# Attention on 128-key value tiles: two ways to lay out keys, weights and sums in one fused kernel

## The chip, the cores and the metric

The kernel runs on one core of a Trainium2 chip. The metric is the device time of one execution in microseconds. Five engines work in parallel, each through its own queue in order: TensorE (PE, with its weight loads listed apart as PEld), VectorE (DVE), ScalarE (ACT), GpSimd (POOL) and SyncE (SP), which here only issues DMA transfers.

## The reference, cut to what matters

Threshold attention over 8 batches of 8 heads, 576 tokens and 64 columns a head, followed by a feed-forward layer with squared ReLU. All is float32.

```python
scale = 1.0 / np.sqrt(q.shape[-1])
scores = scale * np.matmul(q, k.transpose(0, 1, 3, 2))
thresh = np.max(scores, axis=-1, keepdims=True) - tau
scores = np.where(scores >= thresh, scores, -1000000000.0)
attn = np.exp(scores - np.max(scores, axis=-1, keepdims=True))
attn = attn / (np.sum(attn, axis=-1, keepdims=True) + 1e-09)
x = np.matmul(attn, v)          # (B,H,S,D), then to (B*S, H*D) = 4608 x 512
h = np.maximum(x @ w_in, 0.0)   # w_in 512 x 2048
out = h * h @ w_out             # w_out 2048 x 512
```

## The kernel before, in words

The kernel has two stages. The first, about 520 us long, is the attention, and beside it the weights of the layer are loaded and combined. The second is the feed-forward layer, two dense matrix products written as two-level fast multiplication with 7 x 7 block products in place of 8 x 8. The change touches only the first stage.

**Units and periods.** Heads are taken in 32 pairs (`pairs`), the two heads j = 0, 1 of a pair side by side. A unit is 128 queries of a pair: four full units (t = 0 to 3) of 128 rows each, and one unit for every two pairs that holds the last 64 queries of both. That makes 144 units, worked off two at a time, u = 0 (called A) and u = 1 (called B), in 72 periods (`period(p)`, L607). Inside a period every engine's work is issued in the order of a written list: `CONVERTING` (L596) in the periods in which a chunk of the layer's weights is also being converted (33 of them, p = 2 to 34), `PLAIN` (L592) in the others. Since each engine's queue runs in order, this list is the schedule. In PLAIN periods POOL adds the weight sums `s1` and `s2` in between.

**One unit's way.** Queries and keys are loaded in natural layout (`load_q`, `load_k`), and TensorE transposes them (`turn`, L390, step T) into PSUM banks 1 and 4. ACT evicts them (step eT): queries, and the 64 left-over queries, by an ACTIVATE with the scale `qscale` (a [128, 1] operand, minus one eighth; L402), keys by plain copies (L410). `scores` (L423, steps SA and SB) multiplies 64 head columns by 64 queries at a time, on 64 x 64 quarters of the array, into the six banks of `sc`. `softmax` (L439) then issues:

- `top` (L452, DVE): reads 576 scores of one head out of PSUM, multiplies by the constant 1.0, writes them to `s` and accumulates the minimum (the scores are negated, so it is minus the maximum). Steps topA0, topA1, topB0, topB1.
- `least` (L459, POOL): threshold = that minimum + tau, for both heads of a unit (steps leastA, leastB).
- `power` (L462, ACT): exp of the scores into `w`, which is laid out as 9 blocks of 64 keys x 2 heads x 64 keys' columns.
- `mask` (L467, DVE): keeps the weights whose score passes the threshold (a [128, 1] operand) and accumulates their sum. Steps maskA1, maskA0, maskB0, maskB1.
- `over` (POOL, L474) and `inverse` (DVE, L477, step inv): one over the sums, in the period after.

**Values.** The weights must be turned, so that keys lie on partitions. `fill` (L499) transposes 18 blocks (9 for each of the two units; steps V 8 blocks, W 2, U 8), each as two half transposes (L379), into PSUM; `filled` copies them to `wT` with ACT (L523, steps eV, eW, eU). A block has 64 keys of head 0 on partitions 0 to 63 and 64 keys of head 1 on partitions 64 to 127; keys are taken as 9 consecutive per partition row. In step W, eight small matmuls (L515) against the identity also spread the inverse sums over 64 partitions each. `values` (L525, step PV) multiplies: for each of 9 key chunks, each unit and each head, 64 keys x 64 columns of `v` by 128 queries, on 64 x 64 quarters of the array; head 0 accumulates in bank 0, head 1 in bank 5, unit u in partitions 64u to 64u + 63. A float32 matmul runs as two passes, so 36 matmuls of a period show as 72. `given_out` (step x, L638) multiplies the result by the spread inverse sums on DVE, frees the `v` tile (`load_v` then fetches that of three pairs on) and hands `x` to SP, which writes it to DRAM (L578).

**What orders PE against DVE.** `touch` (L354) adds a dependency wherever two engines use one PSUM bank. So PV, which writes banks 0 and 5, waits for topA0 and topA1 of its period; topA0 waits for T, which writes banks 1 and 4 between SA and topA0; SA waits for eT of the period before.

Of the kernel before, what the change touches and what calls it, by code (L numbers as in the profile page):

```python
# [48 lines left out]
def kernel(  # L49
# [249 lines left out]
    def load_k(i):  # L299
# [4 lines left out]
        for j in range(2):  # L304
            queue = nc.scalar if i == 0 and j == 0 else nc.sync
            keys = k[b, h + j, :, :].rearrange("(p c) d -> p c d", c=CH)
            for e in range(2):
                queue.dma_start(
                    out=kn[ds(e * HALF, HALF), :, ds(j * D, D)],
                    in_=keys[:, ds(e * FULL, FULL), :],  # L310
                )
# [3 lines left out]
            queue.dma_start(out=rn[REST:P, ds(j * D, D)], in_=keys[:, CH - 1, :])  # L315
        queue = nc.sync if i else nc.scalar
        queue.dma_start(
            out=rn[0:REST, :].rearrange("p (j d) -> p j d", j=2),
            in_=q[b, h : h + 2, MAIN:S, :].rearrange("j p d -> p j d"),
        )  # L320
        loaded[i, 1], loaded[i, 2] = kn, rn

    def load_v(i):
        b, hp = pairs[i]
        h = 2 * hp
        va = sb.tile([P, CH, D], FP32, tag="va", bufs=3, name="va")
        nc.sync.dma_start(
            out=va[:, :, :].rearrange("p c d -> p (c d)"),
            in_=v[b, h : h + 2, :, :].rearrange("j (p c) d -> (j p) (c d)", c=CH),
        )  # L330
        loaded_v[i] = va
# [58 lines left out]
    def turn(i, which, spots, other=None):  # L390
# [10 lines left out]
        def scaled(to, spot):  # L401
            touch("turned", nc.scalar.activation(out=to, in_=spot[0], func=AF.Identity, scale=qscale[:, :]), spot[1], BANK, i)  # L402

        def then():
            part = lambda r, x, n: (spots[r][0][:, ds(x, n)], spots[r][1])
            if which:
                for r, n in ((0, half), (1, half + REST)):
                    spot = part(r, 0, n)
                    copy_by = other if r and other else nc.scalar.copy
                    touch("turned", copy_by(to[1][:, ds(r * half, n)], spot[0]), spot[1], BANK, i)  # L410
                scaled(to[2], part(0, half, REST))
                next_keys(i)
            else:
                for r in range(2):
                    scaled(to[0][:, ds(r * half, half)], part(r, 0, half))
# [23 lines left out]
    def softmax(n):  # L439
# [8 lines left out]
        of = lambda j: s[:, j, :].rearrange("p (c d) -> p c d", d=D)  # L448

        def top(j):  # L450
            at = 3 * j * BANK + (n % 2 != j) * (2 * BANK - REST)
            made = nc.vector.tensor_scalar(  # L452
                out=s[:, j, :], in0=sc[:, ds(at, S)], scalar1=1.0, scalar2=None,
# [7 lines left out]
        def power(j):  # L461
            nc.scalar.activation(  # L462
                out=w[:, :, j, :], in_=of(j), func=AF.Exp, bias=nmx[:, j : j + 1], scale=-1.0
            )

        def mask(j):
            nc.vector.scalar_tensor_tensor(  # L467
                out=w[:, :, j, :], in0=of(j), scalar=thr[:, j : j + 1], in1=w[:, :, j, :],
# [23 lines left out]
    FIRST = [(u, c) for c in range(CH) for u in range(2)]  # L492
    FILLS = {"V": (0, 8), "W": (8, 2), "U": (10, 8)}
    SCALE_AT = 10

    def weight_at(n):
        return n if n < SCALE_AT else n + 2

    def fill(m, f, pt, at=None):  # L499

        first, count = FILLS[f]
        if m not in wT:
            wT[m] = sb.tile([P, (2 * CH + 2) * P], FP32, tag="wT", bufs=W_RING, name="wT")
        for i, (u, c) in enumerate(FIRST[first : first + count]):
            half_turn(pt, i, weights[2 * m + u][:, c, :, :].rearrange("p j d -> p (j d)"), at)
        if f == "W":
            rs = smalls.pop(m)
            for j in range(2):
                for r in range(2):
                    rows = ds(r * HALF, HALF)  # L510
                    for u in range(2):
                        one = rs[rows, 3, 2 * u + j : 2 * u + j + 1]
                        wide = bass.AP(tensor=one.tensor, offset=one.offset, ap=[one.ap[0], [0, D]])
                        to = pt[ds(u * D, D), r, ts(count + j, HALF)]
                        made = nc.tensor.matmul(to, wide, ident[rows, rows], start=True, stop=True)  # L515
                        touch("turns", made, at and at + r * BANK, BANK)

    def filled(m, f, pt, at=None):

        first, count = FILLS[f]  # L520
        count += 2 * (f == "W")
        to = wT[m][:, ds(weight_at(first) * P, count * P)]
        touch("weights", nc.scalar.copy(joined(to), whole(pt, 0, count)), at, 2 * BANK, m)  # L523

    def values(m):  # L525

        for c in range(CH):
            for u in range(2):
                for s, (i, _, count, row) in enumerate(halves(2 * m + u)):
                    for j in range(2):  # L530
                        rows = ds(j * D, D)
                        made = nc.tensor.matmul(  # L532
                            sc[ds(u * D, D), ds(5 * j * BANK + row, count)], loaded_v[i][rows, (c - (u != j)) % CH, :],
                            wT[m][rows, ds(weight_at(2 * c + u) * P + row, count)],
                            start=(c == 0 and s == 0), stop=(c == CH - 1), skip_group_check=True,
                        )
                        touch("values", made, 5 * j * BANK, BANK, m)
# [672 lines left out]
```

## Time and profile before

| what | value |
|---|---|
| timed runs | 1318.28, 1319.75, 1321.89 us; median 1319.75 |
| profiled execution | span 1314.0 us from first to last instruction; the page gives no time around it, and the median of the timed runs lies 5.8 us above |
| granted TensorE clock | 0.998 |
| PE / DVE / ACT / POOL busy over the span | 97% / 77% / 65% / 64% |
| DVE busy, 35.55 to 264.31 us (31 converting periods) | 225.2 of 228.8 us |
| DVE busy, 264.31 to 507.47 us (37 periods, nearly all plain) | 234.2 of 243.2 us |
| PE busy in the same two stretches | 210.8 and 239.6 us |

The two stretches are bounded by reciprocals (L477), of which there is one a period: 35.55, 264.31 and 507.47 us are starts of such instructions. Busy times count the spans of instructions, and neighbours on one engine overlap a little; where a price is wanted, the distance from one start to the next in the timeline is the better measure. Matmul ends are modelled, so a busy PE alone does not say that PE is the limit.

### The profile page before, as it was taken

Reading aid. Unit: us, or ns where it says so; the run is one execution under the profiler, and the core shown is the slowest. Engines: PE = TensorE matmul, PEld = TensorE weight load, DVE = VectorE, ACT = ScalarE, POOL = GpSimd, SP = SyncE. Lnnn points to the kernel's source line nnn. Section 1 sums busy time; section 2 is a strip of 40 time slices with the busy share of each in tenths; the row PEclk is TensorE's granted clock in tenths of the full one; section 3 lists DMA queues with packets and bytes.
Section 4 is the critical chain, followed back from the end, with each engine's and each line's share of the span. In section 5 each row is a group of like instructions: output and inputs, shape, how many; then the busy total and the mean of one; then the engine's idle time right before and its main releaser. Section 6 shows DMA issues by size and latency. Waiting matters only on the chain.

```text
span 1314.0 us, 47792 instructions
## 1 busy us (share of the span) xinstructions
PE 1277.6 (97%) x19483; PEld 1141.4 (87%) x19483; DVE 1016.3 (77%) x2497; ACT 849.6 (65%) x1464; POOL 839.0 (64%) x958
## 2 busy tenths in 40 slices
PE   7999999899999999999999999999999999999998
PEld 5666666677777777999999999999999999999998
DVE  5999999999999996877887788777656654665463
ACT  5999999888989886566756675665524322432240
POOL 1444444455555421778987888758777777777775
PEclk9999999999999999999999999999999999999999
DMA  5555566544433322466656655669645135423411
GB/s 135 143 160 142 155 174 182 149 103 99 101 78 86 77 60 46 148 206 192 195 180 210 197 187 179 193 232 394 249 161 161 48 115 162 161 63 100 161 33 33
DMA packets 247035, 192.12 MB, mean 146 GB/s; under 512 B 97184, under 2 KB 195488, under 8 KB 246816
## 3 DMA queue, kind: packets, MB, share of 16 engines
q1 hardware_dynamic: 245360, 188.63, 47.4%
q8 instruction: 153, 2.51, 0.8%
q10 hardware_dynamic: 1456, 0.44, 0.1%
q14 instruction: 66, 0.54, 0.1%
HBM read 116.65 MB, written 72.35 MB: 144 GB/s over the span
## 4 chain that ended last, share of the span: by engine, by line
PE 85%; ACT 8%; DVE 3%; issue 2%; DMA 1%; SPq 1%; POOL 0%; ACTq 0%; DVEq 0%; POOLq 0%
PE ph L812 30%; PE po L947 28%; PE sc L434 9%; PE sc L532 8%; PE pt L379 5%; ACT arena L523 3%; ACT arena L462 3%; PE sc L397 2%; PE sc L515 2%; DVE arena L452 1%; PE sc L379 1%; DMA wall<-w 1%; ACT arena L402 1%; DVE arena L467 0%; DMA arena<-in_k_dram 0%
## 5 line engine op out<-in xcount | busy, mean ns | idle before, releaser
L125 POOL TENSOR_TENSOR arena<-arena 128x512 f32<-128x512 f32 (+1 forms) x314 | 378.0, 1222 | 134.5 <-DVE arena L125 120.5
L947 PE MATMUL po<-wall,arena 128*128 128x128 f32 x3528 | 395.0, 275 | 1.6 <-ACT arena L724 1.4
L947 PEld LDWEIGHTS po<-wall,arena 128*128 128x128 f32 x3528 | 394.3, 192 | 2.2 <-ACT arena L724 1.8
L812 PE MATMUL ph<-arena,wall 128*128 128x128 f32 x3528 | 394.2, 275 | 0.7 <-DVE arena L638 0.7
L812 PEld LDWEIGHTS ph<-arena,wall 128*128 128x128 f32 x3528 | 394.0, 192 | 0.8 <-issue 0.8
L125 DVE TENSOR_TENSOR arena<-ph,arena 128x512 f32<-128x512 f32 x378 | 256.4, 689 | 86.2 <-PE ph L812 66.0
L122 POOL TENSOR_TENSOR arena<-arena 128x128 f32<-128x128 f32 (+2 forms) x314 | 255.2, 814 | 48.6 <-DMA arena<-w 31.9
L125 DVE TENSOR_TENSOR arena<-po,arena 128x128 f32<-128x128 f32 x378 | 108.4, 290 | 167.6 <-PE po L947 163.4
L467 DVE SCALAR_TENSOR_TENSOR arena<-arena 128x576 f32<-128x576 f32 x288 | 229.6, 817 | 2.7 <-ACT arena L462 1.7
L462 ACT ACTIVATE arena<-arena 128x576 f32<-128x576 f32 x288 | 208.2, 778 | 14.1 <-DVE arena L452 7.0
L452 DVE TENSOR_SCALAR_CACHE_REDUCE arena<-sc 128x576 f32<-128x576 f32 x288 | 205.5, 751 | 13.3 <-ACT arena L523 5.5
L758 ACT COPY c<-arena 128x512 f32<-128x512 f32 (+1 forms) x303 | 173.5, 579 | 50.4 <-DVE arena L122 41.3
L532 PEld LDWEIGHTS sc<-arena 64*64 64x64 f32 x5760 | 154.0, 133 | 55.3 <-DVE arena L452 28.7
L532 PE MATMUL sc<-arena 64*64 64x128 f32 (+1 forms) x5760 | 176.7, 263 | 18.1 <-DVE arena L452 11.6
L122 DVE TENSOR_TENSOR arena<-arena,c 128x512 f32<-128x512 f32 (+1 forms) x267 | 174.9, 663 | 6.1 <-ACT c L758 4.0
L434 PE MATMUL sc<-arena 64*64 64x64 f32 (+1 forms) x2304 | 167.4, 414 | 5.6 <-ACT arena L402 5.6
L523 ACT COPY arena<-pt 128x1024 f32<-128x1024 f32 x144 | 146.6, 1018 | 24.8 <-PE pt L379 24.4
L724 ACT COPY arena<-po 128x128 f32<-128x128 f32 x63 | 16.6, 264 | 186.4 <-PE po L947 183.7
L459 POOL TENSOR_SCALAR arena<-arena,tau_p 128x2 f32<-128x2 f32 x144 | 75.1, 521 | 73.4 <-DVE arena L452 67.8
L724 ACT COPY arena<-ph 128x512 f32<-128x512 f32 x63 | 36.6, 581 | 124.2 <-PE ph L812 123.5
L379 PEld LDWEIGHTS pt<-ident,arena 64*128 64x128 f32 x2304 | 83.1, 139 | 38.2 <-ACT arena L523 25.6
L434 PEld LDWEIGHTS sc<-arena 64*64 64x64 f32 x2304 | 59.2, 134 | 52.2 <-ACT arena L402 26.4
(46 smaller groups left out, 896.1 us busy)
## 6 DMA issues: line engine op xcount, KB each, us to landing
g<-arena SPq DMA_DIRECT2D x144, 256.0 KB, 2.4
arena<-g SPq DMA_DIRECT2D x144, 256.0 KB, 4.4
w<-arena SPq DMA_DIRECT2D x60, 256.0 KB, 2.4
wall<-w SPq DMA_DIRECT2D x49, 256.0 KB, 5.2
arena<-w SPq DMA_DIRECT2D x44, 256.0 KB, 3.2
arena<-in_v_dram SPq DMA_DIRECT2D x32, 288.0 KB, 3.6
out_dram<-arena SPq DMA_DIRECT2D x70, 128.0 KB, 2.2
arena<-in_q_dram SPq DMA_DIRECT2D x64, 128.0 KB, 3.2
```

The source lines that it names most:

```text
L122: e.tensor_tensor(out=out, in0=x, in1=y, op=ALU.subtract)
L125: e.tensor_tensor(out=out, in0=x, in1=y, op=ALU.add)
L379: made = nc.tensor.transpose(pt[:, r, ts(slot, HALF)], of[rows, :], ident[rows, rows])
L434: made = nc.tensor.matmul(sc[at, ds(to, count)], lhs, kT[rows, ds(at_k, count)], start=True, stop=True)
L452: made = nc.vector.tensor_scalar(out=s[:, j, :], in0=sc[:, ds(at, S)], scalar1=1.0, scalar2=None, op0=ALU.mult, op1=ALU.min, accum_out=nmx ...
L462: nc.scalar.activation(out=w[:, :, j, :], in_=of(j), func=AF.Exp, bias=nmx[:, j : j + 1], scale=-1.0)
L467: nc.vector.scalar_tensor_tensor(out=w[:, :, j, :], in0=of(j), scalar=thr[:, j : j + 1], in1=w[:, :, j, :], op0=ALU.is_le, op1=ALU.mult, a ...
L523: touch("weights", nc.scalar.copy(joined(to), whole(pt, 0, count)), at, 2 * BANK, m)
L532: made = nc.tensor.matmul(sc[ds(u * D, D), ds(5 * j * BANK + row, count)], loaded_v[i][rows, (c - (u != j)) % CH, :], wT[m][rows, ds(weigh ...
L758: nc.scalar.copy(c, y)
L812: nc.tensor.matmul(to[:, j, :], W_IN[m, k][:, ts(j, P)], of[k][:, m - 1, :], start=(not more and j == 0), stop=True, skip_group_check=True,)
L947: nc.tensor.matmul(to, g[:, j, :], w[:, j, :], start=(not more and j == 0), stop=(j == 3), skip_group_check=True)
```

## The change

Five things change together, all in the attention stage.

- **Keys over 128 partitions.** `load_k` loads keys 0 to 511 of a head as 4 consecutive keys for each of 128 partitions, in one DMA a head; the last 64 keys of both heads go beside the last 64 queries. ACT's evictions of the turned keys interleave two PSUM banks. `load_v` loads `v` in the same order: two DMAs for the main part and two for the last 64 keys, which are loaded twice, on both partition halves.
- **Weights laid out by head.** `w` is 2 heads x 576 keys, contiguous; which head comes first depends on the unit, so that the last 64 keys of both heads meet in one block of 128 columns.
- **Values of 128 keys by 64 columns.** A period turns 16 blocks of 128 keys of one head and 2 blocks with the rests of both. `values` multiplies 128 keys x 64 columns by 128 queries, on the left or right 64 columns of the array by head; the rests go on 64 x 64 quarters, in the middle (order 0, 1, rest, 2, 3). Unit u now has its own bank (0 or 5) and head j its partitions. For a period of two full units: 16 + 4 matmuls instead of 36. `x` is 128 x 256, and neighbouring query blocks of a pair go to DRAM in one DMA.
- **Sums spread by transposes of a widened copy.** A new step `spread`, right behind `inv`, has POOL write the four inverse sums of a period 64 times over (`widen`, 128 x 256); W turns these two blocks with the two rest blocks. The eight matmuls of L515 go. U stays 8 blocks, V 8, W becomes 4.
- **Scores scaled in the maximum pass.** ACT's evictions of queries are plain copies, and `top` multiplies by `qscale`, a [128, 1] operand, in place of the constant 1.0.

```diff
-        units.append(((i, i + 1), FULL))
+        units.append(((i, i + 1) if i % 4 == 0 else (i + 1, i), FULL))
...
+            queue.dma_start(
+                out=kn[:, :, ds(j * D, D)], in_=k[b, h + j, 0:MAIN, :].rearrange("(p t) d -> p t d", t=FULL)
+            )
...
+        for rows, x in ((ds(0, REST), k), (ds(REST, REST), q)):
+            queue.dma_start(
+                out=rn[rows, :].rearrange("p (j d) -> p j d", j=2),
+                in_=x[b, h : h + 2, MAIN:S, :].rearrange("j p d -> p j d"),
+            )
...
+        for j in range(2):
+            nc.sync.dma_start(
+                out=va[:, j, :, :], in_=v[b, h + j, 0:MAIN, :].rearrange("(p t) d -> p t d", t=FULL)
+            )
+        for e in range(2):
+            nc.sync.dma_start(
+                out=vr[ds(e * REST, REST), :, :], in_=v[b, h : h + 2, MAIN:S, :].rearrange("j p d -> p j d")
+            )
...
-            touch("turned", nc.scalar.activation(out=to, in_=spot[0], func=AF.Identity, scale=qscale[:, :]), spot[1], BANK, i)
+        def evicted(by, to, spot, first, n):
+            made = by(to, spot[0][:, ds(first, n)].rearrange("p (t q) -> p t q", q=HALF))
+            touch("turned", made, spot[1], BANK, i)
...
-        w = sb.tile([P, CH, 2, D], FP32, tag="w", bufs=4, name="w")
+        w = sb.tile([P, 2, S], FP32, tag="w", bufs=4, name="w")
...
-                out=s[:, j, :], in0=sc[:, ds(at, S)], scalar1=1.0, scalar2=None,
+                out=s[:, j, :], in0=sc[:, ds(at, S)], scalar1=qscale[:, :], scalar2=None,
...
-    FILLS = {"V": (0, 8), "W": (8, 2), "U": (10, 8)}
+    FILLS = {"V": (0, 8), "W": (16, 4), "U": (8, 8)}
...
+    def widen(m):
+        if m not in wT:
+            wT[m] = sb.tile([P, (SCALE_AT + 2) * P], FP32, tag="wT", bufs=W_RING, name="wT")
+        one = smalls.pop(m)[:, 3, 0:1]
+        wide = bass.AP(tensor=one.tensor, offset=one.offset, ap=[one.ap[0], [1, 4], [0, D]])
+        nc.gpsimd.tensor_copy(out=wT[m][:, ds(SCALE_AT * P, 2 * P)].rearrange("p (x d) -> p x d", d=D), in_=wide)
...
-        for c in range(CH):
+        for n, c in enumerate((0, 1, FULL, 2, 3)):
             for u in range(2):
                 for s, (i, _, count, row) in enumerate(halves(2 * m + u)):
                     for j in range(2):
+                        va, vr = loaded_v[i]
+                        if c < FULL:
+                            lhs, rhs = va[:, j, c, :], wT[m][:, ds((4 * c + 2 * j + u) * P + row, count)]
+                        else:
+                            rows = ds((u != j) * REST, REST)
+                            lhs, rhs = vr[rows, j, :], wT[m][rows, ds((TAIL + u) * P + row, count)]
                         made = nc.tensor.matmul(
-                            sc[ds(u * D, D), ds(5 * j * BANK + row, count)], loaded_v[i][rows, (c - (u != j)) % CH, :],
+                            sc[ds(j * D, D), ds(5 * u * BANK + row, count)], lhs, rhs,
...
-        inv powA0 c5 topB1 powB1 eT maskA1 x W eV maskA0 leastB c2 c6 eW maskB0 maskB1
+        inv spread powA0 c5 topB1 powB1 eT maskA1 x W eV maskA0 leastB c2 c6 eW maskB0 maskB1
...
-        leastB inv powA0 PV powB0 W maskA0 x powB1 maskB0 T c4 c5 maskB1 eT V c6 eW eV
+        leastB inv spread powA0 PV powB0 W maskA0 x powB1 maskB0 T c4 c5 maskB1 eT V c6 eW eV
```

More of the change, by code (lines that the diff above doesn't have):

```diff
@@ L544, in valued @@
             if units[n][1] == FULL:
-                for i in units[n][0]:
+                for i in sorted(units[n][0]):
                     loaded_v.pop(i)
@@ L550, in give_x @@
     def give_x(m, x):
[L552 to L557 removed]
+        for i, first, count, at in parts_of(m, lambda x, y: (x[0], x[1] + x[2]) == y):
+            b, hp = pairs[i]
+            given.append((xT[b][ds(hp * P, P), ds(first, count)], x[:, ds(at, count)]))
     def has(n):
@@ L673, in period @@
         }
+        steps["spread"] = lambda: has(2 * m + 2) and widen(m + 1)
         steps["over"] = lambda: do(a, "over")
```

101 lines of the change are left out of this document (39 added, 62 removed).

## The prediction, made before the result was known

> **What bounds the kernel now.** I read the page first, then busy time by stage, the groups by shape, and two stretches of the timeline.
>
> ```profile
> span 1314.0 us, 47792 instructions
> PE   7999999899999999999999999999999999999998
> DVE  5999999999999996877887788777656654665463
> ```
>
> PE is busy everywhere, but in the first 16 slices, the attention, DVE is as full. The change touches only these slices, so the rest of the span stays. The busy time of the two attention stretches (PE, PEld, DVE, ACT, POOL, then clock, DMA share, GB/s) tells them apart:
>
> ```profile
> 35.55:264.31 228.76, 210.78 (x5358) 146.01 (x5352) 225.22 (x654) 215.25 (x349) 102.25 (x156) 1.00 0.57 157
> 264.31:507.47 243.16, 239.59 (x6310) 179.94 (x6306) 234.21 (x702) 216.83 (x337) 118.04 (x168) 1.00 0.35 83
> ```
>
> The first holds 31 converting periods, 7.38 us each: DVE is busy for 98% and PE for 92%. The second holds 37 periods of 6.57 us: PE 99%, DVE 96%. Both engines matter, and the timeline must say which ends last. First the prices by group and shape (busy, mean ns, idle before):
>
> ```profile
> L467 DVE SCALAR_TENSOR_TENSOR arena<-arena 128x576 f32<-128x576 f32 x288 | 229.6, 817 | 2.7 <-ACT arena L462 1.7
> L452 DVE TENSOR_SCALAR_CACHE_REDUCE arena<-sc 128x576 f32<-128x576 f32 x288 | 205.5, 751 | 13.3 <-ACT arena L523 5.5 <-PE sc L397 2.0 <-ACT arena L212 1.7
> L235 DVE SCALAR_TENSOR_TENSOR arena<-arena 128x512 int32<-128x512 int32 x32 | 22.3, 698 | 1.1
> L402 ACT ACTIVATE arena<-sc,qscale 128x256 f32<-128x256 f32 x62 | 25.6, 463 | 4.2 <-PE sc L397 4.2
> L410 ACT COPY arena<-sc 128x256 f32<-128x256 f32 x32 | 11.6, 361 | 6.2 <-PE sc L397 6.2
> ```
>
> A converting period in the timeline (start, length); the distance between starts is what an instruction costs DVE:
>
> ```profile
> 147.77 0.70 DVE L235 SCALAR_TENSOR_TENSOR arena<-arena 128x512 int32<-128x512 int32 x1
> ...
> 148.38 0.82 DVE L467 SCALAR_TENSOR_TENSOR arena<-arena 128x576 f32<-128x576 f32 x1
> ...
> 149.12 0.76 DVE L452 TENSOR_SCALAR_CACHE_REDUCE arena<-sc 128x576 f32<-128x576 f32 x1
> ...
> 149.80 0.76 DVE L452 TENSOR_SCALAR_CACHE_REDUCE arena<-sc 128x576 f32<-128x576 f32 x1
> ```
>
> A top costs 0.68, a mask 0.74, L235 0.61; by the same view L227 costs 0.46, the two x multiplies 0.40, the reciprocal 0.09. A converting period's DVE work is 4 x 0.68 + 4 x 0.74 + 0.46 + 0.61 + 0.40 + 0.09 = 7.24 us of 7.38: DVE sets these periods. A plain one has 6.17 us of DVE work. There:
>
> ```profile
> 387.45 0.76 DVE L452 TENSOR_SCALAR_CACHE_REDUCE arena<-sc 128x576 f32<-128x576 f32 x1
> ...
> 388.13 0.75 DVE L452 TENSOR_SCALAR_CACHE_REDUCE arena<-sc 128x576 f32<-128x576 f32 x1
> 388.30 0.13 PEld L532 LDWEIGHTS sc<-arena 64*64 64x64 f32 x1 [0.28 <-DVE arena L452]
> 388.73 2.16 PEld L532 LDWEIGHTS sc<-arena 64*64 64x64 f32 x71 [0.30 <-issue]
> ...
> 390.45 0.81 DVE L467 SCALAR_TENSOR_TENSOR arena<-arena 128x576 f32<-128x576 f32 x1
> 390.63 0.79 POOL L459 TENSOR_SCALAR arena<-arena,tau_p 128x2 f32<-128x2 f32 x1
> 391.07 0.57 PEld L379 LDWEIGHTS pt<-ident,arena 64*128 64x128 f32 x16 [0.17 <-issue]
> ...
> 391.56 0.20 PEld L379 LDWEIGHTS sc<-ident,arena 64*128 64x128 f32 x4
> ...
> 391.83 0.32 PEld L515 LDWEIGHTS sc<-ident,arena 64*64 64x64 f32 x16
> ...
> 393.96 0.76 DVE L452 TENSOR_SCALAR_CACHE_REDUCE arena<-sc 128x576 f32<-128x576 f32 x1
> ```
>
> This is a loop: topA0, topA1, the value products (which wait for both), V, W, SA, T, and the next topA0, 387.45 to 393.96 = 6.51 us, mostly PE. DVE has 0.34 us to spare in it.
>
> **The change part by part.**
>
> *Scale in top.* L452 gets a [128, 1] operand. No such DVE instruction out of PSUM is in the trace. From below: nothing, if its fetch hides behind the PSUM read; no reason gives a gain. From above: ACT's L402 with such an operand against L410 without, both 128x256 out of PSUM, 463 - 361 = 0.10 us. Between: on DVE, L467 has the operand and L235, of the same kind, has a constant; beyond 1.04 ns an element (L125 on DVE: 689 ns at 512, 290 at 128), so 0.60 and 0.53 us, they cost 0.14 and 0.08 from start to start. I take 0.06: same engine, and 0.10 is another's. That is +0.24 us of DVE work a period, 0.12 of it (topA0, topA1) on the plain loop. The Trainium skill, "ScalarE: Activation LUTs", section What ACT_TABLE_LOAD costs, gives about 93 ns for each pointer operand of an ACTIVATE, as L402 and L410 agree; as an estimate for DVE it would put the sum about 6 us higher, but that page speaks of ACT.
>
> *Query evictions as copies.* Two of 463 become 361, and the 64-query one (324) falls likewise: about 0.3 us less ACT a pair. ACT is on the path only where scores wait for the eviction itself: one plain period in nine takes 7.09 us (356.64 to 363.73) since PE waits 0.41 for L402. There it gives back 0.2. Key evictions move as many columns.
>
> *Value products.* 72 passes ran on quarters, four together: 2.16 us for 18 slots of 0.12. After, 32 passes on half arrays go two together and 8 on quarters four together: again 18 slots. A slot of full rows is in the trace: L812, 3528 passes in 394.2 us, 0.112. So no gain by the count. The first waits fall otherwise: before, the second product already writes bank 5 and waits for topA1; after, two slots go to bank 0 first: -0.16. New are two changes of array shape, into the rests and out. PEld's idle time at such changes is 0.17 (before V at 391.07) and 0.07 (391.76 to 391.83, before L515); I take 0.12 each, between them: +0.24. Entering PV is hidden by its wait for topA1. The Trainium skill, "TensorEngine Tiling (Array Packing)", Key Properties, says that changing the tiling mode drains the engine; the 0.17 agrees in kind, and a full drain is a rival below.
>
> *Sums.* L515's 16 weight loads take 391.83 to 392.06 = 0.23 off W and a shape change 0.07, four more half transposes add 4 x 0.036 (16 in 0.57), and the change back to quarters moves to SA: W goes from 0.50 (391.56 to 392.06) to 0.36, -0.14. POOL gets `spread`, 128x256. Prices: not under 0.23 (L474, 128x4), not over 0.61 (L219, 128x512, one input); about 0.4, half way. It must end before W's last blocks and stands ahead of leastB, for which maskB0 waits. leastB at 390.63 took 0.79, against 0.29 elsewhere, because it began under maskA1. After, in plain periods with two weight sums (44 sums on `wall`, so 22 periods), the second sum ends 0.12 later, at 390.75; spread begins under maskA1 (390.69 to 391.43), ends near 391.8, and leastB then meets maskA0 (391.83 to 392.57) and ends near 392.8, while DVE wants maskB0 at 392.57. I take 0.25 of DVE wait there; the ends are 0 and leastB's full 0.79. In converting periods leastB comes first, and spread can delay only W, where PE has 0.5 us to spare.
>
> *Loads and stores.* Costed at nothing. SP issues ten transfers a pair before and after (keys 7 to 4, values 1 to 4), stores fall from 20 to 13 per four pairs, at 0.6 each; the issues of 36 to 264 us sum to 167 us, so SP has room, and values are fetched three pairs ahead. Where that cover fails, it is a key load: one 7.44 us period now ends on one. Contiguous `w`: ACT and DVE move as many elements. Not counted: neither L467 nor L462 shows a price for runs.
>
> *Sum.* Converting: DVE work 7.24 + 0.24 = 7.48; of today's 0.14 of waits I keep 0.05, as ACT gets lighter: 7.53, +0.15, for 33 periods +5.0. Plain, ordinary (29 periods): loop 6.51 + 0.12 - 0.16 + 0.24 - 0.14 = 6.57, +0.06, +1.7; DVE work is 6.41, and with leastB's wait 6.66, +0.09 more in 22 periods, +2.0. Four periods without a turn run at 6.23 to 6.29 and cannot fall under 6.41: +0.6. The four late ones: +0.12 - 0.21, -0.4. Total +8.9: span 1323; outside it stay the 5.8 us by which the median 1319.75 exceeds it: 1329.
>
> **Rivals.**
>
> *The operand is free (faster).* Place: the four tops; price 0 in place of 0.06; under about 0.02 this case decides. Converting 7.24 + 0.05: -3.0. Plain 6.45, leastB's wait no longer binding (6.17 + 0.25): -1.7, late periods -0.8. Together -5.5: 1314. For it: the trace has no such DVE read of PSUM, and a fetch from SBUF could run beside it. Against: L402 reads PSUM too and pays.
>
> *No measurable change.* Spread slips in ahead of the masks and a shape change costs 0.07: plain 6.47, -1.2 - 0.4 - 0.4 + 0.6, and half of converting's price lost in today's waits, +3: 1321. For it: in 15 plain periods POOL has no second sum.
>
> *Full drains.* Each of the two changes costs a whole matmul, 0.27 (L532's 274 ns), not 0.12: +0.30 in 33 periods, +10: 1339. This is the drain rule named above at its dearest. Against: L515 started 0.07 after its predecessor's loads.
>
> *Half arrays don't run side by side, or their loads aren't hidden.* 16 more slots of 0.112, +1.8 us: plain +66, converting (PE 6.8 to 8.6) +36: over 1420. Against: four quarters do run together, and L812's loads of all rows (394.0 us) hide fully. The skill's "TensorE: Matmul & The Clock Gate", The mechanism, lets loads overlap only where row groups differ; L812 speaks against its biting here.
>
> **How the numbers follow.** Forecast 0.41, free operand 0.20, no change 0.22, full drains 0.12, no overlap 0.05. The bound for telling a change is 0.3%, 4 us: 1315.8 and 1323.7. Faster: the free operand's 0.20. Same: 0.22 and the forecast's lower edge, 0.05: 0.27. Slower: the rest, 0.53. Range: the free operand with cheap shape changes (0.10 less, 33 times, -3.3) gives 1311, full drains with 3 us more for a dearer operand 1342; outside lie no overlap and the tails. The forecast's own range is 1323 to 1336.
>
> **What would show it.** L452's mean near 811 and starts 0.74 apart; L402's line at 361; converting periods of 7.5 us; plain ones of 6.6, with L467 idle before maskB0 on POOL L459; PV's 40 passes as long as 72 were, with a gap on either side of the rests. Tops still 0.68 apart, or value passes 0.112 apart singly, would make it wrong.

## The result, and the profile after

| | before | after |
|---|---|---|
| median of the timed runs | 1318.78 us (1315.46 to 1322.49) | 1321.76 us (1318.88 to 1327.33) |
| span of the profiled execution | 1314.0 us | 1317.1 us |
| 31 converting periods | 228.76 us | 231.92 us |
| 37 plain periods | 243.17 us | 244.02 us |
| ahead of them | 35.55 us | 34.91 us |

The ratio is 1.0023, 95% interval [1.0012, 1.0034]: 3 us slower, where 9 were forecast. Of the 3.1 us by which the span grew, converting holds +3.16, plain +0.85, the start -0.64 and all the rest -0.3. After has 40,939 instructions in its span, 6,900 fewer. The busy time of the two attention stretches of after (PE, PEld, DVE, ACT, POOL, then clock, DMA share, GB/s):

```profile
34.91:266.82 231.91, 206.47 (x3870) 137.85 (x3868) 230.16 (x652) 211.81 (x349) 129.03 (x187) 1.00 0.55 153
266.82:510.85 244.03, 241.82 (x4566) 163.25 (x4564) 239.72 (x704) 214.61 (x336) 134.33 (x205) 1.00 0.34 86
```

In converting DVE went from 225.2 to 230.2 us while the stretch grew by only 3.2: its waits shrank. PE lost 4.3 us of work there, to no effect on the time. In plain DVE gained 5.5 us and PE 2.2, and the stretch grew by 0.85. The groups of after, by shape (busy, mean ns of one | idle before):

```profile
L468 DVE SCALAR_TENSOR_TENSOR arena<-arena 128x576 f32<-128x576 f32 x288 | 228.5, 814 | 0.8 <-ACT arena L463 0.7
L453 DVE TENSOR_SCALAR_CACHE_REDUCE arena<-sc,qscale 128x576 f32<-128x576 f32 x288 | 221.8, 812 | 8.4 <-PE sc L399 2.1 <-issue 1.8 <-ACT arena L212 1.6
L404 ACT COPY arena<-sc 128x256 f32<-128x256 f32 x93 | 31.1, 368 | 7.1 <-PE sc L399 7.1
L512 POOL COPY arena<-arena 128x256 f32<-128x256 f32 x72 | 55.0, 764 | 11.9 <-DVE arena L478 8.1 <-PE sc L551 0.9
```

The top (L453, was L452) went from 751 to 812 ns, the 0.06 of the forecast, while the masks (L468) stayed at 814. Evictions of 128 x 256, queries and keys in one group now, take 368 ns; queries took 463. The copy of the sums (L512) takes 764 on average, where 0.4 us was taken. A plain period of after in the timeline:

```profile
390.18 0.82 DVE L453 TENSOR_SCALAR_CACHE_REDUCE arena<-sc,qscale 128x576 f32<-128x576 f32 x1
...
390.92 0.81 DVE L453 TENSOR_SCALAR_CACHE_REDUCE arena<-sc,qscale 128x576 f32<-128x576 f32 x1
391.51 0.92 PEld L551 LDWEIGHTS sc<-arena 128*64 128x64 f32 x16 [0.81 <-DVE arena L453]
...
392.60 0.21 PEld L551 LDWEIGHTS sc<-arena 64*64 64x64 f32 x8 [0.17 <-issue]
392.98 0.85 PEld L551 LDWEIGHTS sc<-arena 128*64 128x64 f32 x16 [0.17 <-issue]
...
393.24 0.82 DVE L468 SCALAR_TENSOR_TENSOR arena<-arena 128x576 f32<-128x576 f32 x1
393.31 1.00 POOL L512 COPY arena<-arena 128x256 f32<-128x256 f32 x1
...
394.00 0.58 PEld L381 LDWEIGHTS pt<-ident,arena 64*128 64x128 f32 x16 [0.17 <-PE sc L551]
...
394.30 0.29 POOL L460 TENSOR_SCALAR arena<-arena,tau_p 128x2 f32<-128x2 f32 x1
394.38 0.81 DVE L468 SCALAR_TENSOR_TENSOR arena<-arena 128x576 f32<-128x576 f32 x1
...
395.11 0.82 DVE L468 SCALAR_TENSOR_TENSOR arena<-arena 128x576 f32<-128x576 f32 x1
...
396.79 0.82 DVE L453 TENSOR_SCALAR_CACHE_REDUCE arena<-sc,qscale 128x576 f32<-128x576 f32 x1
```

The loop runs from 390.18 to 396.79, 6.61 us (6.51 in the period shown of before). The value products end with the transposes of V at 394.00, 2.49 us after they began. On either side of the rests PE's loads stand 0.17 idle, waiting for nothing that the profile shows; these are the places where the array shape changes. The tops start 0.74 apart. And maskB0, at 395.11, does not wait: leastB ended at 394.59.

The lengths of single periods, from one reciprocal to the next, tell more than sums. Converting: before, most lie between 7.19 and 7.45, often 7.20 and 7.33 in turn (a period that transposes keys, then one that transposes queries); after, 28 of 31 lie between 7.43 and 7.47. Plain periods come in a pattern of nine (us, in order; the second has no turn, the last waits for the query eviction):

| | 1 | 2 | 3 | 4 | 5 | 6 | 7 | 8 | 9 |
|---|---|---|---|---|---|---|---|---|---|
| before | 6.50 | 6.29 | 6.68 | 6.51 | 6.45 | 6.51 | 6.58 | 6.50 | 7.09 |
| after | 6.47 | 6.49 | 6.62 | 6.55 | 6.61 | 6.54 | 6.68 | 6.54 | 6.96 |

### The profile page after: what moved, and what is told of

The parts are those of the page before. It is cut to its first block, busy times and chain, and to the rows that moved or that the text cites. A ratio compares the mean times of both kernels' runs of the same rounds, so it can differ in the third digit from the quotient of the medians.

```text
span 1317.1 us, 40939 instructions
## 1 busy us (share of the span) xinstructions
PE 1275.0 (97%) x16059; PEld 1116.0 (85%) x16059; DVE 1027.7 (78%) x2497; ACT 843.7 (64%) x1464; POOL 883.7 (67%) x1030
## 4 chain that ended last, share of the span: by engine, by line
PE 82%; DVE 8%; ACT 5%; issue 2%; POOL 1%; DMA 1%; DVEq 0%; POOLq 0%; ACTq 0%
PE ph L828 30%; PE po L963 29%; PE sc L436 9%; PE sc L551 8%; PE pt L381 4%; DVE arena L453 4%; DVE arena L468 3%; ACT arena L463 3%; PE sc L399 1%; POOL arena L512 1%; PE sc L381 1%; ACT arena L526 1%; DVE arena L235 1%; DMA wall<-w 1%; ACT arena L404 1%
## 5 line engine op out<-in xcount | busy, mean ns | idle before, releaser
L468 DVE SCALAR_TENSOR_TENSOR arena<-arena 128x576 f32<-128x576 f32 x288 | 228.5, 814 | 0.8 <-ACT arena L463 0.7
L453 DVE TENSOR_SCALAR_CACHE_REDUCE arena<-sc,qscale 128x576 f32<-128x576 f32 x288 | 221.8, 812 | 8.4 <-PE sc L399 2.1
L551 PEld LDWEIGHTS sc<-arena 128*64 128x64 f32 (+1 forms) x3200 | 141.5, 135 | 72.7 <-DVE arena L453 45.3
L551 PE MATMUL sc<-arena 128*64 128x128 f32 (+3 forms) x3200 | 184.5, 272 | 11.7 <-DVE arena L453 10.6
L460 POOL TENSOR_SCALAR arena<-arena,tau_p 128x2 f32<-128x2 f32 x144 | 65.9, 458 | 65.5 <-DVE arena L453 61.5
L436 PEld LDWEIGHTS sc<-arena 64*64 64x64 f32 x2304 | 58.6, 134 | 53.3 <-issue 24.8
```

The costliest lines, as they stand in the source:

```text
L436: made = nc.tensor.matmul(sc[at, ds(to, count)], lhs, kT[rows, ds(at_k, count)], start=True, stop=True)
L453: made = nc.vector.tensor_scalar(out=s[:, j, :], in0=sc[:, ds(at, S)], scalar1=qscale[:, :], scalar2=None, op0=ALU.mult, op1=ALU.min, accu ...
L468: nc.vector.scalar_tensor_tensor(out=w[:, int(n % 2 != j), :], in0=s[:, j, :], scalar=thr[:, j : j + 1], in1=w[:, int(n % 2 != j), :], op0 ...
L551: made = nc.tensor.matmul(sc[ds(j * D, D), ds(5 * u * BANK + row, count)], lhs, rhs, start=(n == 0 and s == 0), stop=(n == FULL), skip_gro ...
```

## The experiments

The theory going in was the forecast's: DVE's work sets the converting periods, so the operand of the tops is their price, and the shape changes that of the plain ones. Its rival: something else, the copy of the sums above all, holds the time up. Ratios are to the kernel before, on the same chip; stretches are of one profiled execution each. In nearly every profile some converting periods between 155 and 260 us are longer than the others by 0.3 to 3.4 us, other ones each time, and the stretch ahead of the converting periods varies by up to 3.7 us. So readings rest on single periods first; sums over the converting stretch carry that noise, those over the plain one hardly.

**The operand undone (e1_scale_back), and alone (e2_scale_only).** In e1, after's tops multiply by 1.0 again and ACT scales the queries:

```diff
+        def scale(to, spot):
+            return nc.scalar.activation(out=to, in_=spot, func=AF.Identity, scale=qscale[:, :])
...
-                    evicted(nc.scalar.copy, part, spots[r], 0, half)
+                    evicted(scale, part, spots[r], 0, half)
...
-                out=s[:, j, :], in0=sc[:, ds(at, S)], scalar1=qscale[:, :], scalar2=None,
+                out=s[:, j, :], in0=sc[:, ds(at, S)], scalar1=1.0, scalar2=None,
```

> The changed kernel with one part undone: scores scaled in ACT's query evictions again, the maximum pass multiplies by the constant 1.0. Theory (each engine's own work decides: converting periods follow DVE's work, plain periods follow PE's chain): L453's starts go from 0.74 back to 0.68 us apart; converting periods fall from 7.48 to 7.3 us on average, -0.1 to -0.2 in 33 periods, so -3 to -6 us against the changed kernel; ordinary plain periods stay at 6.55 to 6.6, because PE has no wait left in them, and the plain period that waits for a query eviction grows by 0.2, +1 us in all. Together -2 to -5 us against the changed kernel, about level with the kernel before. Rival (PE's waits for the widened copy, 31 us in the converting stretch, set the converting periods): these stay at 7.44 or more and the time does not fall.

In e2, before has this one part of the change and no other:

```diff
-            touch("turned", nc.scalar.activation(out=to, in_=spot[0], func=AF.Identity, scale=qscale[:, :]), spot[1], BANK, i)
+            touch("turned", nc.scalar.copy(to, spot[0]), spot[1], BANK, i)
...
-                out=s[:, j, :], in0=sc[:, ds(at, S)], scalar1=1.0, scalar2=None,
+                out=s[:, j, :], in0=sc[:, ds(at, S)], scalar1=qscale[:, :], scalar2=None,
```

> The kernel before with one part of the change alone: the maximum pass multiplies by the [128, 1] scale, ACT's query evictions become copies. Theory (DVE's work decides the converting periods, and the two maximum passes at the head of the value products lie on the plain loop): converting 7.38 to 7.46, +2.5 to 3 us in 33 periods; ordinary plain periods 6.51 to 6.57 or 6.63, +2 to 4 us; the late ones 7.09 to 7.0; periods without a turn 6.25 to 6.41. Together +4 to +7 us against the kernel before. Rival (plain periods are PE's alone also in the kernel before, and the wait for the maximum passes has slack): plain unchanged, +2 to 3 us in all.

Measured: e2 1.0034 [1.0022, 1.0046], e1 1.0018 [1.0009, 1.0027]. Alone the operand costs what it should (converting 7.43 to 7.44, evenly; plain 6.57 in place of 6.51 in the commonest period, 246.1 us in sum), but taking it back gives next to nothing: converting sums to 233.2 us, against 231.9 with it, and two long periods (8.99 and 8.75) are in that sum. Its ordinary periods now alternate, 7.20 and 7.65; their mean of 7.43 is 0.02 or 0.03 under after's. So in every second period something other than DVE's work sets the length: the theory falls for e1. The timeline of e1 around such a pair (L515 is the copy of the sums here, L404 the key eviction):

```profile
149.66 0.80 POOL L515 COPY arena<-arena 128x256 f32<-128x256 f32 x1
...
150.52 0.20 PEld L381 LDWEIGHTS sc<-ident,arena 64*128 64x128 f32 x4 [0.52 <-POOL arena L515]
150.52 0.34 PE L381 MATMUL sc<-ident,arena 64*128 64x64 f32 x4 [0.38 <-POOL arena L515]
...
151.20 0.70 ACT L404 COPY arena<-sc 128x320 f32<-128x320 f32 x2 [0.79 <-PE sc L399]
...
156.94 0.93 DVE L471 SCALAR_TENSOR_TENSOR arena<-arena 128x576 f32<-128x576 f32 x1 [0.24 <-ACT arena L466]
```

W waits for the copy; T stands behind W in PE's order; ACT idles 0.79 for T, and its queue is late from there on; in the next period maskA0 waits 0.24 for an exponential. In the waits of e1's converting stretch (us in total, times, longest) that last link comes up 15 times:

```profile
DVE arena L471 <- ACT arena L466: 4.9, 15, 1.3
```

After has the first links too, and not the last one, as its waits over the same stretch show:

```profile
PEld sc L381 <- POOL arena L512: 17.6, 30, 0.6
ACT arena L404 <- PE sc L399: 15.7, 27, 0.9
DVE arena L468 <- ACT arena L463: 0.4, 1, 0.4
```

The new theory, tested next, is that the dearer tops keep DVE busy just long enough to hide this second chain. Two things differ between e1 and after, and the timelines part them. In a period that turns keys, ACT's next exponentials begin 6.78 us after the reciprocal in e1 (149.32 to 156.10) and 6.66 in after (146.94 to 153.60): evictions without the scale account for 0.12. DVE wants the first of them 7.30 after it in e1 and 7.53 in after: the tops account for 0.23.

**The chain cut: T ahead of W (e5_turn_first, e10_after_turn_first, e8_spread_turn_first, e9_before_turn_first), and the spread alone (e6_spread_only).** If T does not stand behind the wait, ACT is not late. e5 is e1 with one step of the list moved; e10 is after with the same move:

```diff
-        leastB inv spread powA0 PV powB0 W maskA0 x powB1 maskB0 T c4 c5 maskB1 eT V c6 eW eV
+        leastB inv spread powA0 PV powB0 T W maskA0 x powB1 maskB0 c4 c5 maskB1 eT V c6 eW eV
```

> The changed kernel with the scale back in ACT's query evictions, as in the first of these runs, and in the converting list the turn T ahead of W. Theory (in converting periods PE stands before W until POOL has written the widened copy; T, its eviction by ACT and the next scores queue behind that, and with the slower scaled eviction this chain, 7.65 us in periods that turn queries, outlasts DVE's 7.2): with T ahead these periods fall to 7.2 to 7.35, 16 of them, -5 us against the run without this step, and the time comes to 0.997 to 0.999 of the kernel before. Rival (ACT's own work in these periods makes 7.65): they stay, and the time with them.

> The changed kernel with T ahead of W in the converting list. Theory (with the scale in the maximum pass converting periods stand on DVE's 7.45 us of work, so that PE's wait for the copy is covered): they stay at 7.44 to 7.47, only those of 7.7 fall to 7.45, -1 us; 1.001 to 1.002 of the kernel before. Rival (the wait for the copy is what the change costs in converting periods): they fall to 7.2, -7 us.

e5: ordinary converting periods 7.19 to 7.21, in both kinds, the stretch 4.6 us below e1; 0.9993 [0.9982, 1.0005]. e10: 7.43 to 7.45, as after, 231.8 us; 1.0029 [1.0018, 1.0040]. Both expectations were a little too good in time, and right in the periods. So with the operand DVE's own work is the limit, and without it the copy's wait is.

e6 is before with the spread alone (a copy on POOL and two transposed blocks in W in place of L515):

```diff
+        one = rs[:, 3, 0:1]
+        wide = bass.AP(tensor=one.tensor, offset=one.offset, ap=[one.ap[0], [1, 2], [2, 2], [0, D]])
+        to = wT[m][:, ds(SCALE_AT * P, 2 * P)].rearrange("p (j u d) -> p j u d", j=2, d=D)
+        nc.gpsimd.tensor_copy(out=to, in_=wide)
...
-                        made = nc.tensor.matmul(to, wide, ident[rows, rows], start=True, stop=True)
-                        touch("turns", made, at and at + r * BANK, BANK)
+                half_turn(pt, count + j, wT[m][:, ts(SCALE_AT + j, P)], at)
...
+        steps["spread"] = lambda: has(2 * m + 2) and widen(m + 1)
```

> The kernel before with one part alone: the sums spread by POOL's widened copy and transposes, in place of the eight small matmuls. Theory: in converting periods PE waits before W for the copy, and since the scale is still in ACT's evictions the periods that turn queries rise from 7.34 to 7.6, +4 us; in plain periods V and W get 0.15 shorter on the loop and the entry to SA 0.05 longer, -0.1 in 29 periods, -3 us. Together +1 us, within 0.3%. Rival (the wait for the copy is hidden): converting periods stay at 7.38, together -3 us.

Measured: 1.0022 [1.0013, 1.0031]; converting 7.28 and 7.66 in turn, 233.5 us, +4.7 against before; plain 242.6, -0.55. The copy's wait is in this part by itself. In plain the expectation missed: a shorter W took 0.15 off one place of the pattern (6.43 in place of 6.58) and 0.11 off the one without a turn, but the four places at 6.50 and 6.51 stayed there. Two lines of such a period of before, and one of e6, show why:

```profile
386.28 0.53 PEld L434 LDWEIGHTS sc<-arena 64*64 64x64 f32 x16 [0.45 <-ACT arena L402]
387.99 1.01 ACT L523 COPY arena<-pt 128x1024 f32<-128x1024 f32 x1 [0.37 <-PE pt L379]
...
390.49 0.42 PEld L434 LDWEIGHTS sc<-arena 64*64 64x64 f32 x16 [0.56 <-ACT arena L402]
```

In such a period ACT is busy all the time but for 0.06 and these 0.37 us, in which PE turns the blocks of U (from 387.18 on; ACT had finished eV at 387.13). PE stands 0.45 before the scores until ACT has evicted what T turned; in the other ordinary periods the gap there is 0.28. With a shorter W it only stands longer, 0.56. So in four of nine places ACT's own queue sets the length, and not the value products and W. The floor is the same 6.50 or 6.51 in every kernel here in which ACT scales the queries, wherever nothing longer hides it, and 6.47 where its evictions are copies (after's first place, and e12), with the same 0.38 idle.

e8 is e6 with T ahead of W, and e9 is before with T ahead of W and nothing else:

```diff
-        leastB inv powA0 PV powB0 W maskA0 x powB1 maskB0 T c4 c5 maskB1 eT V c6 eW eV
+        leastB inv powA0 PV powB0 T W maskA0 x powB1 maskB0 c4 c5 maskB1 eT V c6 eW eV
```

> The kernel before with the widened copy and its transposes alone, and T ahead of W in the converting list. Theory: PE no longer holds T back for the copy, so converting periods stay at 7.2 to 7.4, and plain periods gain 0.1: 0.996 to 0.998 of the kernel before, faster than both kernels. Rival (POOL's copy delays something else in converting periods, or plain periods are not PE's): no gain.

> The kernel before with T ahead of W in the converting list and nothing else: the control for the run that had this step and the widened copy. Theory (the step pays in the kernel before too, since W waits there for the reciprocal and T behind it): converting periods that turn queries fall from 7.33 to 7.2, those of 7.6 likewise, -3 to -4 us, and the copy's own share of that run's gain, from plain periods, is 1 us or less: 0.997 to 0.998 of the kernel before. Rival (that run's gain needs the widened copy): 0.9995 to 1.0005.

e8: 0.9973 [0.9963, 0.9983], 1314.43 us; e9: 0.9973 [0.9961, 0.9984], 1314.65 us. These two are the fastest kernels here, faster than both before and after, and the whole gain is the moved step: before's own converting periods held the same chain in a weaker form (ACT's L410 idle 0.30 for L397 at 147.03, and maskA0 at 152.78, 0.20 after the reciprocal's start and not 0.09). The two attention stretches of e9:

```profile
36.39:262.79 226.40, 209.05 (x5364) 145.86 (x5360) 223.33 (x652) 215.08 (x349) 101.94 (x156) 1.00 0.58 160
262.79:506.03 243.24, 239.73 (x6302) 179.84 (x6298) 234.72 (x702) 216.38 (x336) 117.81 (x168) 1.00 0.36 83
```

Converting is 2.4 us under before's, plain the same, and ordinary converting periods take 7.19 to 7.21: DVE's work, counted from the prices as 7.24, is really 7.19.

**The values alone (e7_values_only).** After with ACT scaling the queries and the eight matmuls spreading the sums:

```diff
-    FILLS = {"V": (0, 8), "W": (16, 4), "U": (8, 8)}
+    FILLS = {"V": (0, 8), "W": (16, 2), "U": (8, 8)}
...
+                        wide = bass.AP(tensor=one.tensor, offset=one.offset, ap=[one.ap[0], [0, D]])
+                        to = pt[ds(j * D, D), r, ts(count + u, HALF)]
+                        made = nc.tensor.matmul(to, wide, ident[rows, rows], start=True, stop=True)
...
-        inv spread powA0 c5 topB1 powB1 eT maskA1 x W eV maskA0 leastB c2 c6 eW maskB0 maskB1
+        inv powA0 c5 topB1 powB1 eT maskA1 x W eV maskA0 leastB c2 c6 eW maskB0 maskB1
```

> The changed kernel with two parts undone: scale in ACT's evictions, sums spread by the eight small matmuls. What is left of the change is the layout of keys, weights and values, with products of 128 keys by 64 columns. Theory: converting periods as in the kernel before, 7.33 to 7.4; the value products cost 0.05 to 0.1 us more on the plain loop for their changes of array shape, +2 to +4 us in all. Rival (fewer and fuller products pay): plain periods fall and the time with them, by 2 us or more.

Measured: 1.0035 [1.0022, 1.0047]; converting periods 7.20 and 7.36, nearly as before; plain 246.0, +2.8: the commonest period 6.59 in place of 6.51, those without a turn 6.59 in place of 6.29. The new layout costs the commonest plain period 0.08, and converting periods next to nothing.

**The shape changes (e3_rest_first, e4_both, e11_more_shapes, e12_rest_last).** The rests' place in the order of the value products was moved in after. First, in e3 (and in e4, which is e3 with e1's edit):

```diff
-        for n, c in enumerate((0, 1, FULL, 2, 3)):
+        for n, c in enumerate((FULL, 0, 1, 2, 3)):
```

> The changed kernel with the products of the rests first (order rest, 0, 1, 2, 3) in place of the middle: one change of array shape inside the value products and none on entering them, in place of two and one. Theory (each change of shape costs PE 0.15 us and PE's chain sets the plain periods): the value products of a plain period take 2.25 us in place of 2.5; ordinary plain periods fall from 6.57 to the floor of DVE's work, 6.39 to 6.45, -4 to -6 us; converting periods, on DVE's floor, stay at 7.48. Rival (changes of shape cost nothing and the value products are long for the waits for the maximum passes): no change, within 1 us.

> The changed kernel with both: rests first, and the scale back in ACT's query evictions. Theory: DVE's work falls to 6.15 us a plain period and PE's chain to about 6.3, so ordinary plain periods come to 6.3 to 6.4 us, -0.2 in 29 periods, and converting periods to 7.25 to 7.35: -8 to -13 us against the changed kernel and -5 to -10 against the kernel before, which it would beat. Rival (the plain loop is bound by ACT's chain of evictions and exponentials, not by PE): plain periods stay above 6.5 and the sum is that of the scale alone, -2 to -5.

Last, in e12:

```diff
-        for n, c in enumerate((0, 1, FULL, 2, 3)):
+        for n, c in enumerate((0, 1, 2, 3, FULL)):
```

> The changed kernel with the products of the rests last: one change of array shape fewer, and the two slots that lie ahead of the wait for the second maximum pass stay. Theory: ordinary plain periods fall by 0.1 to 0.15, to 6.45 to 6.5, near DVE's 6.4, -3 to -5 us; converting periods unchanged. Rival (plain periods are set by ACT's chain): within 1 us.

Split, in e11:

```diff
-        for n, c in enumerate((0, 1, FULL, 2, 3)):
-            for u in range(2):
+        order = [(c, u) for c in (0, 1) for u in range(2)] + [(FULL, 0)]
+        order += [(2, u) for u in range(2)] + [(FULL, 1)] + [(3, u) for u in range(2)]
+        for c, u in order:
```

> The changed kernel with the rests of the two units apart, unit 0 after chunk 1 and unit 1 after chunk 2: four changes of array shape inside the value products in place of two, the same products. Theory (a change costs PE 0.15 us and PE's chain sets the plain periods): the value products get 0.3 us longer, ordinary plain periods rise from 6.58 to 6.85, +8 to +11 us; converting periods unchanged. Rival (changes of shape cost nothing): no change.

e3: 1.0022 [1.0012, 1.0031], e4: 1.0010 [0.9998, 1.0022]. With the rests first one change is saved, and yet the ordinary plain period went from 6.55 to 6.61. The products of unit 1 wait for topA1; in after, two slots of unit 0 are done before it (391.51 to 391.80), in e3 only unit 0's rests, which fill half a slot each, and the two full slots come after the wait. What was saved in shape was lost in cover: a miss of the expectation, which had weighed the changes alone. e4 differs from e3 by e1's edit; its converting periods alternate 7.20 and 7.65 as e1's. Its expectation missed as well, and the rival named there came true: its commonest plain periods stay at 6.50 to 6.52, which is ACT's floor.

e12: 1.0018 [1.0005, 1.0030], in time not told apart from after. It keeps the two slots ahead of the wait and saves one change: plain 241.4 us, 2.6 under after, with the commonest periods 6.47 in place of 6.55; there they stand on ACT's floor. Converting is 233.1, 1.2 above after, with every second period near 7.55; the cause is open.

e11: 1.0202 [1.0179, 1.0225], converting 242.1 and plain 260.4 us. Most of the 10 us in converting lies in six long periods (8.12 to 10.87), whose cause is open; the plain ones are the measure. The rests in its value products, in the timeline:

```profile
386.28 0.19 PEld L553 LDWEIGHTS sc<-arena 64*64 64x64 f32 x4 [0.17 <-issue]
386.65 0.42 PEld L553 LDWEIGHTS sc<-arena 128*64 128x64 f32 x8 [0.17 <-issue]
387.23 0.20 PEld L553 LDWEIGHTS sc<-arena 64*64 64x64 f32 x4 [0.17 <-issue]
387.60 0.42 PEld L553 LDWEIGHTS sc<-arena 128*64 128x64 f32 x8 [0.17 <-issue]
```

The loads stand 0.17 idle four times in place of two, and the commonest plain period of 7.05 in place of 6.55: +0.50. Two causes share it. In the starts of single matmuls, in after, successive slots of one shape lie 0.109 apart; the first slot after a change starts 0.21 after the one ahead and the next follows 0.16 later: (0.21 - 0.109) + (0.16 - 0.109) = 0.15 a change. Two more make 0.30. The other 0.22 is two slots: the rests of one unit alone fill two of the four quarters, so four slots run where two did, which the expectation had missed. Together 0.52.

## Why the prediction was right and wrong

The forecast was +8.9 us in the span, and +3.1 came. Of the 5.8 between them, 2.0 is a wait that did not come (DVE for leastB), 1.5 the 31 converting periods, and 0.9 the ordinary plain ones; the rest is in the late plain periods, the start and the end.

**The tops, right.** 0.06 each: 751 to 812 ns, starts 0.74 apart. The rival of a free operand is out.

**Converting, over-sized.** "Of today's 0.14 of waits I keep 0.05", 7.53 us, +5.0. It came to 231.92 / 31 = 7.48, +3.16. The number that failed is the DVE work: it is 0.05 less than the prices sum to (e9 runs at 7.19, not 7.24), so that 0.19 of before's 7.38 were waits, not 0.14. With 7.19 + 0.24 = 7.43 the 0.05 that was kept gives the 7.48 that came; 28 of 31 periods have 0.02 of it on average, and three longer ones (7.71, 7.72, 7.90) the rest. The reason, "as ACT gets lighter", is the smaller part: e5 and e9 have the heavy query evictions and no such waits, once T is out of the way. The waits are those of a chain through W, T and ACT, which the longer tops cover by 0.23 and lighter evictions shorten by 0.12. Of the tops' 0.24 some 0.14 only took the place of these waits.

**The wait for leastB, wrong, and the largest miss.** Forecast 0.25 in 22 periods, +2.0; measured none: no wait of DVE for POOL is in either stretch of after. The copy was indeed held up by maskA1, and more than thought (1.00 us). But the failing sentence is "leastB then meets maskA0": the two x multiplies lie between the masks (0.40 us), and in the period shown the copy ended at 394.31, 0.33 and not 0.4 after DVE's next instruction began (393.98), and leastB, in POOL from 394.30, was ahead of maskA0 (394.38) by 0.08 and took 0.29, not 0.79. The trace of after holds the other order too. In its last 12 plain periods, which have no second weight sum, the copy runs ahead of maskA1 in 0.40 and leastB takes 0.79 under it; they are as long as the same places of the pattern with the copy at 1.00 (6.49 and 6.49, 6.62 and 6.62, 6.55 and 6.55). Neither order costs DVE a wait. The order that was forecast, leastB behind the start of maskA0, is in no plain period here, so its price stays unmeasured.

**The plain loop, right in its number and wrong in its path.** Forecast 6.57, +0.06 each; measured in the 29 ordinary periods 0.84 us in all, +0.03 each. The step that failed is "ACT is on the path only where scores wait for the eviction itself: one plain period in nine": ACT's queue sets four more of the nine. There W's -0.14 bought nothing (e6: 6.51 as before), and lighter evictions, put at nothing in these periods, lowered the floor from 6.51 to 6.47. In the commonest period the tops alone cost 0.06 (e2: 6.57), where 0.12 was in the sum; the new layout alone costs the 0.08 of -0.16 + 0.24 (e7). Two terms that were too large, of opposite sign, cancelled, which is partly luck. The shape changes are 0.15 each, 0.30 together, where 0.24 was summed. The forecast's range for a shape change (0.07 to 0.17) holds it. Full drains of 0.27, the third rival, are excluded: e11's two more changes would have added 0.54, where 0.28 is left beside the two slots. The rule of the Trainium skill, "TensorEngine Tiling (Array Packing)", Key Properties, that a change of the tiling mode drains the engine, agrees with these gaps in kind.

**Periods without a turn and late ones.** The four without a turn gained 0.89 us in all (forecast 0.6): 6.29 to 6.49, above the 6.41 that was their floor by DVE: e7, with the new layout and no dearer tops, has 6.59 there, so PE's part of the change is on them too. Three of the late ones fell by 0.13 or 0.14, and the fourth, the 7.44 one, by 0.48; -0.9 in all (forecast -0.4). In the fourth a further wait of 0.42 before a top (303.93 in before), which the forecast put down to a key load, is gone. e7 has lost it too (7.09), e6 and e9 have not (7.44), so it went with the new layout.

**Loads and stores at nothing, right** but for that one wait: no new wait that costs time names one.

**The half arrays, right.** Pairs of 128-row products run side by side, one pair in 0.109 us, and their loads hide. By the starts of single matmuls the quarters of before took 0.109 a slot too; the 0.12 of the sum holds their waits. The last rival (over 1420) is out.

**What the sum did not see.** The three parts alone make 0.34% (e2), 0.35% (e7) and 0.22% (e6), 0.9% if they were added; together they make 0.23%. Converting shows why: the operand raises DVE's chain to 7.44, the spread raises the chain over POOL, PE and ACT to about 7.47 on average (7.28 and 7.66), and a period costs the larger one, not the sum. In plain the parts make +2.9 (e2), +2.8 (e7) and -0.55 (e6), 5.2 if they were added, and the change makes 0.85. The spread takes 2.5 off the new layout (e7's 246.0 against e1's 243.5), which had lifted the periods above ACT's floor, and only 0.55 off the old one; and the operand adds 0.55 to e1, where ACT gets lighter at the same time, and 2.9 to before. The prediction weighed the copy in converting against PE's 0.5 us of slack alone ("spread can delay only W"); the T behind W, and ACT behind T, were not in it. By itself that wait is worth 4.7 us (e6), and the dearer tops happened to hide it. The rival of no measurable change gave 1321, where the time is. But that was +1.6 on a median of 1319.75, and before's median over 14 runs is 1318.78, so that the measured difference is 3.0. Of its three premises only the third held (half of converting's price lost in waits), while the copy did not slip in ahead of the masks in most plain periods and a shape change costs 0.15, not 0.07. That its number fits is largely luck.

Open: why e12's converting periods are longer, and where the 0.6 us of the start went (it varies by more between kernels).

## What to carry to other kernels

Price each chain through a period from end to end, in every kind of period, and take the largest: ACT, third by busy time in the plain stretch (216.8 us, against 239.6 and 234.2), still set four periods in nine, and a shorter W there only lengthened PE's wait.

The same holds for experiments: when two chains lie within 0.2 us of each other, undoing one edit shows the other chain and not the edit's price, so measure each part alone as well as taken away. Before adding a producer to a slow engine, look at what stands in order behind the instruction that will wait for it (here T behind W); moving that one step ahead gained 0.27%, where none of the three parts gained anything by itself. An extra operand or an array-shape change of 0.06 to 0.15 us counts only on the chain that is the largest, and work that is done while another wait runs is free, so a reordering that saves a change can lose more cover than it gains.

## What the runs showed of the hardware

- A [128, 1] multiplier in place of a constant costs a 128 x 576 top out of PSUM 0.06 us (751 to 812 ns).
- Changing between 128 x 64 and 64 x 64 array shapes costs about 0.15 us each time, 0.10 of it as a later first slot and 0.05 as a slower second one; 128 x 64 halves run in pairs, 0.109 us a pair.
- One POOL copy of 128 x 256 takes 0.40 us when it starts ahead of a mask and 0.8 to 1.0 when it starts under one, ending 0.3 after it; the mask's two inputs are in SBUF. Which comes first decides by less than 0.1 us: leastB took 0.29 as the first and 0.79 as the second. A mask that began 0.08 behind a copy took 0.93 (e1, 156.94), one that began 0.08 behind leastB the usual 0.81. The Trainium skill, "SBUF — State Buffer", Who interferes with whom, has a DVE instruction with two SBUF inputs contend with a GpSimd one that reads SBUF, the first taking the port and the other blocking; the numbers agree.
